# Fused SSM and SwiGLU block: the bulk loads moved to SyncE's queue in another order, the head's transposes spread over PSUM banks

## The chip, the cores and the metric

The kernel runs on one core of a Trainium2 chip. The metric is the device time of one execution in microseconds. A profiled execution gives the span from its first to its last instruction, and the profile's times count from the start of that span.

## The reference

The input x has 2048 rows (tokens) of 512 columns. Its layer norm xn goes into two branches, and the sum of both and of x is the output, in bfloat16:

```python
xn = _layernorm(x, axis=-1)
return x + _A_ref(xn, ...) + _B_ref(xn, w_gate, w_up, w_down)

# _A_ref: a diagonal state-space layer with 512 complex states
B_bar = ((Lam_bar - 1.0) / Lam)[:, None] * Bmat      # Lam_bar = exp(dt * Lam)
Bu = jnp.einsum("bld,pd->blp", x + 0j, B_bar)
h = Lam_bar[None, :] * h + Bu[:, t, :]               # over the 2048 tokens
y = 2.0 * jnp.einsum("blp,dp->bld", hseq, Cmat).real + x * Dskip

# _B_ref: w_gate and w_up are 512 x 1376, w_down is 1376 x 512
(silu(x @ w_gate) * (x @ w_up)) @ w_down
```

## The kernel before

The tokens go in four chunks of 512, each of four tiles of 128. For the matmuls that contract over the 512 columns, TensorE needs xn with columns on partitions: xnT. It is made by DMA transposes from xn, one for each tile of tokens (xT_dma, L242). The recurrence is turned into a real scan: the products with B (bproj_tile, L365, BT as weights, first four groups with the real part, then four with the imaginary part) are rotated by tables of cosines and sines on VectorE (L375 to L389), scanned there (L407), rotated back into wt, and multiplied by CF on TensorE (out_ssm, L562). CF is worked out from C (CT, L348 and L351). The gated branch is made by gate and up matmuls (L440), a product on VectorE (L459), and the down projection (out_ffn, L552, weights wd_sb). The 1376 columns are ten full groups of 128 and 96 last ones, whose weights are the tiles w_last (gate's last columns and 32 of up) and wu_last (the remaining 64 of up); they are used by gateup_last (L491, and for two chunks together in L501).

The head (L647 to L707) deals with chunk 0 before anything is normalised: x is only centred (xc), transposed by TensorE into PSUM (cT_pe, L234) and copied out by ScalarE (cT_copy, L238) as xcT, and gate and up are taken from it with tokens on the output's partitions (sw_mm, L467); the scale rstd is applied when PSUM is read (sw_out, L476 and L477). This gate and up product (g0, which lies in chunk 1's guT buffer) is transposed by four DMAs (g0_dma, L484). The head uses three weight groups, wg0/wu0 (3 x 128 columns), wg1/wu1 (4 x 128) and wg2/wu2 (3 x 128). PSUM tiles of one name take the eight banks in turn, so a ninth waits until the first has been read. tA and tB are the two banks for the head's transposes, each with two halves.

Each engine works through its instructions in the order of the program, and so do the queues that issue DMAs: SyncE's (SP), ScalarE's (ACT) and GpSimd's (POOL). The DMAs issued from SP run on one hardware queue, those from GpSimd on another (q1 and q0 in the profile). In the program's text, work for VectorE is put in a backlog (queue, with a tag and a cost for each operation); after every group of matmuls, pump lets as much of it into the program as its time pays for, and need(tag) puts in all that is left of a tag. So the place of a line in the backlog decides where VectorE's, and with it SP's and GpSimd's, instructions stand: xT_dma of a chunk is issued by the same backlog operation as the tile's norm.

Before the change, SP issues in this order: part of x and weights of group 0, wg1 and wu1, eight transposes for BT, three loads for w_last, xnT of chunk 0, xnT of chunk 1, guT's four transposes, eight for CT. GpSimd issues wg2 and wu2 among its roots for the head (L662, L669), x of chunk 1 (L686), x of chunks 2 and 3 behind chunk 1's statistics (load_x in the backlog, L704), and wu_last and wd_sb behind chunk 2's statistics (load_down, L769).

Of the kernel before, what the change touches and what calls it, by code (L numbers as in the profile page):

```python
# [23 lines left out]
def kernel(  # L24
# [17 lines left out]
    nc = tc.nc  # L42
    _, L, D = A_x.shape
    Pst = A_Lambda_re.shape[0]
    F = B_w_gate.shape[1]
# [3 lines left out]
    NT = L // 128  # L49
    NCH = L // CW  # L50
    TPC = CW // 128
    KD = D // 128
# [6 lines left out]
    LA, LB = 32, 64  # L59
    FL = (FT - 1) * 128  # L60
# [19 lines left out]
    x_v = A_x[0].rearrange("(n p) d -> p n d", p=128)  # L80
    out_v = out[0].rearrange("(n p) d -> p n d", p=128)
    wg_v = B_w_gate.rearrange("(k p) f -> p k f", p=128)
    wu_v = B_w_up.rearrange("(k p) f -> p k f", p=128)


    xall = const.tile([128, NT, D], BF16, name="xall")
# [3 lines left out]
    wg_g, wu_g = [], []  # L90
# [4 lines left out]
    w_last = const.tile([128, KD, 128], BF16, name="w_last")  # L95
# [15 lines left out]
    def load_w1(q, tiles, view, gi):  # L111
        a, b = fgroups[gi]
        q.dma_start(out=tiles[gi][:], in_=view[:, :, a * 128:min(F, b * 128)])


    def load_w1_half(q, tiles, view, gi, k0, k1):
        a, b = fgroups[gi]
        q.dma_start(out=tiles[gi][:, k0:k1, :], in_=view[:, k0:k1, a * 128:min(F, b * 128)])

    HK = KD // 2  # L120
# [7 lines left out]
    nc.scalar.preload_act_table_set("silu_and_others")  # L128
    load_w1_half(nc.sync, wu_g, wu_v, 0, HK, KD)
    nc.sync.dma_start(out=xall[:, 3, :], in_=x_v[:, 3, :])  # L130
    load_w1(nc.sync, wg_g, wg_v, 1)
    load_w1(nc.sync, wu_g, wu_v, 1)
    prm_rows = const.tile([128, 128], BF16, name="prm_rows")
    nc.gpsimd.memset(prm_rows[:], 0.0)
    for i, v in enumerate((A_Lambda_re, A_Lambda_im, A_log_dt)):
        nc.gpsimd.dma_start(out=prm_rows[i * NQ:(i + 1) * NQ, :], in_=v.rearrange("(q j) -> q j", j=128))
    for part, src in enumerate((A_B_re, A_B_im)):
        for k in range(KD):
            nc.sync.dma_start_transpose(out=BT[:, part, k, :], in_=src[:, k * 128:(k + 1) * 128])
    nc.sync.dma_start(out=w_last[:, :, 0:LB], in_=wg_v[:, :, FL + LA:F])  # L140
    nc.sync.dma_start(out=w_last[:, :, LB:LB + LA], in_=wg_v[:, :, FL:FL + LA])
    nc.sync.dma_start(out=w_last[:, :, LB + LA:128], in_=wu_v[:, :, FL:FL + LA])

    def load_x(c0, c1):
        nc.gpsimd.dma_start(out=xall[:, c0 * TPC:c1 * TPC, :], in_=x_v[:, c0 * TPC:c1 * TPC, :])

    def load_down():
        q = nc.gpsimd
        q.dma_start(out=wu_last[:], in_=wu_v[:, :, FL + LA:F])
        q.dma_start(out=wd_sb[:, 0:nfull, :], in_=B_w_down[0:nfull * 128, :].rearrange("(k p) d -> p k d", p=128))  # L150
        if nfull < FT:
            q.dma_start(out=wd_sb[0:LB, nfull, :], in_=B_w_down[FL + LA:F, :])
            q.dma_start(out=wd_sb[LB:LB + LA, nfull, :], in_=B_w_down[FL:FL + LA, :])
# [25 lines left out]
    def ln_stats(n):  # L179
        nc.vector.bn_stats(out=stats[:, n, 0, :], in_=xall[:, n, :])  # L180
        nc.vector.bn_aggr(out=mv[:, n, :], in_=stats[:, n, 0, :])  # L181

    def ln_stats_half(n, h):
        nc.vector.bn_stats(out=stats[:, n, h, :], in_=xall[:, n, h * HW:(h + 1) * HW])
        if h == 1:
            nc.vector.bn_aggr(out=mv[:, n, :], in_=stats[:, n, :, :])
# [41 lines left out]
    tB = bank((128, 2, KD, 128), BF16)  # L228
    warm = bank()

    def cT_pe(i, k0=0, k1=KD):
        tp = (tA, tA, tB, tB)[i][:, i % 2]
        for k in range(k0, k1):
            nc.tensor.transpose(out=tp[:, k, :], in_=xc[:, i, k * 128:(k + 1) * 128], identity=ident[:])  # L234

    def cT_copy(i, k0=0, k1=KD):
        tp = (tA, tA, tB, tB)[i][:, i % 2]
        nc.scalar.copy(out=xcT[:, k0:k1, i * 128:(i + 1) * 128], in_=tp[:, k0:k1, :])  # L238

    def xT_dma(n):  # L240
        c, i = divmod(n, TPC)
# [13 lines left out]
    V = nc.vector  # L255

    def prm_transpose():
        pp = tA[:, 0, 0, :]
        nc.tensor.transpose(out=pp, in_=prm_rows[:], identity=ident[:])
        V.tensor_copy(out=prm[:].rearrange("p t q -> p (t q)"), in_=pp[:, 0:3 * NQ])  # L260

# [77 lines left out]
    def c_ops():  # L339

        ops = []
        for q in range(NQ):
            for part, (one, coef) in enumerate(((0, c2re), (1, nc2re))):
                box = {}

                def pre(q=q, one=one, coef=coef, box=box):
                    box["t"] = ssm.tile([128, D], F32, name="cm", bufs=3)
                    nc.scalar.activation(out=box["t"][:], in_=CT[:, one, q, :], func=ACT.Copy, scale=coef[:, q:q + 1])  # L348

                def op(q=q, part=part, box=box):  # L350
                    V.scalar_tensor_tensor(out=CF[:, part, q, :], in0=CT[:, 1 - part, q, :], scalar=nc2im[:, q:q + 1],  # L351
                                           in1=box["t"][:], op0=ALU.mult, op1=ALU.add)
                ops.append((0.7, op, pre))
        return ops
# [127 lines left out]
    def g0_dma():  # L482
        for i in range(TPC):
            nc.sync.dma_start_transpose(out=gu_tiles[0][:, 0:FT - 1, i * 128:(i + 1) * 128], in_=g0[:, i, :])  # L484
# [3 lines left out]
    def gateup_last(c):  # L488
        ps = bank()
        for k in range(KD):  # L490
            nc.tensor.matmul(ps[:], lhsT=w_last[:, k, :], rhs=xnT[:, k, c * CW:(c + 1) * CW],  # L491
                             start=(k == 0), stop=(k == KD - 1))
        u = up_last[c] = up_p.tile([128, CW], BF16, name="ul", bufs=2)
        nc.scalar.activation(out=gu_tile(c)[0:LB + LA, FT - 1, :], in_=ps[0:LB + LA], func=ACT.Silu)
        nc.scalar.copy(out=u[LB:LB + LA, :], in_=ps[LB + LA:128])
        if c % 2 == 0:
            return
        ps = bank()
        for k in range(KD):
            for i in range(2):  # L500
                nc.tensor.matmul(ps[i * LB:(i + 1) * LB], lhsT=wu_last[:, k, :],  # L501
                                 rhs=xnT[:, k, (c - 1 + i) * CW:(c + i) * CW], start=(k == 0), stop=(k == KD - 1))
        for i in range(2):
            nc.scalar.copy(out=up_last[c - 1 + i][0:LB, :], in_=ps[i * LB:(i + 1) * LB])
            g, u = gu_tiles[c - 1 + i][0:LB + LA, FT - 1, :], up_last[c - 1 + i][0:LB + LA, :]
            products.append(lambda g=g, u=u: V.tensor_tensor(out=g, in0=g, in1=u, op=ALU.mult))
# [70 lines left out]
    def queue(tag, ops, at=None):  # L577
        ops = [[op[0], op[1], op[2] if len(op) > 2 else None, tag] for op in ops]
        if at is None:
            backlog.extend(ops)  # L580
        else:
            backlog[at:at] = ops
# [24 lines left out]
    def need(tag):  # L607

        while any(item[3] == tag for item in backlog):
            step()  # L610
# [6 lines left out]
    def dummy(n, cols):  # L617
        for _ in range(n):
            nc.tensor.matmul(warm[:, 0:cols], lhsT=one.to_broadcast([128, 128]), rhs=one.to_broadcast([128, cols]),
                             start=True, stop=True)  # L620
# [21 lines left out]
    def head_mm(which, i, k0=0, k1=KD):  # L642
        if k0 == 0:
            held[i][which] = bank()
        sw_mm(held[i][which], (G, U)[which], 0, i, k0, k1)
# [4 lines left out]
    center_by_sum(0, 0, HW)  # L650
    center_by_sum(0, HW, D)
    cT_pe(0, 0, HK)
    dummy(1, 128)
    cT_copy(0, 0, HK)
    cT_pe(0, HK, KD)
    dummy(2, 128)
    cT_copy(0, HK, KD)
    center(1, sums[:, 1:2])
    head_mm(0, 0, 0, HK)
    ln_stats(1)  # L660
    ln_rstd(1, 2)
    load_w1(nc.gpsimd, wg_g, wg_v, 2)  # L662
    cT_pe(1)
    cT_copy(1)
    head_mm(0, 0, HK, KD)
    ln_stats(2)
    center(2, mv[:, 2, 0:1])
    ln_rstd(2, 3)
    load_w1(nc.gpsimd, wu_g, wu_v, 2)  # L669
    head_mm(1, 0, 0, HK)  # L670
    ln_stats_half(0, 0)
    head_mm(0, 1)
    head_mm(1, 0, HK, KD)
    cT_pe(2)
    cT_copy(2)
    ln_stats(3)
    center(3, mv[:, 3, 0:1])
    ln_rstd(3, 4)
# [4 lines left out]
    exp_pool(dt_t[:], ldt)  # L683
    nc.gpsimd.iota(out=jidx[:], pattern=[[1, CW]], base=0, channel_multiplier=0,
                   allow_small_or_imprecise_dtypes=True)
    load_x(1, 2)  # L686
    V.tensor_scalar(out=rs0[:], in0=rstd[:, 0:1], scalar1=1.0 / D, scalar2=None, op0=ALU.mult)
    head_mm(0, 2)
    cT_pe(3)
    cT_copy(3)  # L690
    head_mm(1, 2)
    for n in range(TPC):
        norm_dve(n)
        xT_dma(n)
    params_a()
    head_mm(0, 3)
    sw_out(0, 0, *held[0])
    head_mm(1, 3)
    sw_out(0, 1, *held[1])
# [1 line left out]
    tables = table_ops()  # L701
    stats1, norm1 = ln_rest(1, False)
    queue("tables", tables[:2])
    queue("ln1", stats1 + [(0.0, lambda: load_x(2, NCH))])  # L704
    queue("tables", tables[2:6])
    queue("ln1", norm1)
    queue("tables", tables[6:])  # L707
    ln_nb(0, TPC)
    multiply(0)
    for gi in (1, 2):  # L710
# [55 lines left out]
    fwd0, back0 = ssm_ops(0)  # L766
    stats2, norm2 = ln_rest(2, True)
    queue("ssm0", fwd0[0:2] + [(1.5, params_b)])
    queue("ln2", stats2 + [(0.0, load_down)])  # L769
    queue("ssm0", fwd0[2:6])  # L770
    spread(fwd0[6:] + back0, norm2, "ssm0", "ln2")
    queue("cf", c_ops())
    g0_dma()
    gateup_last(0)
    pump(GU / 2)
    for part, src in enumerate((A_C_re, A_C_im)):
# [62 lines left out]
```

## Time and profile before

| | us |
|---|---|
| three runs, median (lowest to highest) | 191.83 (189.07 to 194.75) |
| the profiled execution | 190.17 |
| its span | 188.3 |
| TensorE busy in the span | 175.5 (93%) |
| VectorE busy | 158.2 (84%) |
| ScalarE busy | 109.3 (58%) |
| GpSimd busy | 33.3 (18%) |

Matmuls overlap one another, so the sum of TensorE's busy time is not a time at its peak rate; what can be read directly are the stretches in which it has nothing to do. In the rows of a timeline the first number is the start, the second the length, then the engine, the line, the operation with what it writes and reads, and in brackets the idle time of the engine before it and what ended it. SPq, ACTq and POOLq are the instructions that issue DMAs. In the rows on DMAs the last number is the median time from issue to landing.

### The profile page before, as it was taken

How to read it: one execution, taken by the hardware profiler on the slowest of the kernel's cores; microseconds unless marked ns; L12 is line 12 of the kernel's file. 1: busy time of each engine (PE TensorE's matmuls, PEld its weight loads, DVE VectorE, ACT ScalarE, POOL GpSimd, SP SyncE). 2: the span in 40 equal slices, each digit the busy share in tenths (PEclk: the TensorE clock that was granted, in tenths of full speed). 3: DMA queues.
4: the chain of work that ended last, by engine and by line, in shares of the span. 5: the costliest groups of instructions: out<-in, count | busy, mean ns of one | idle time of the engine just before them, and what ended most of it. 6: DMA issues, size and time to landing. Idle time of an engine off the chain costs nothing.

```text
span 188.3 us, 2432 instructions
## 1 busy us (share of the span) xinstructions
PE 175.5 (93%) x865; PEld 81.4 (43%) x865; DVE 158.2 (84%) x258; ACT 109.3 (58%) x186; POOL 33.3 (18%) x44
## 2 busy tenths in 40 slices
PE   7999969990799999999999999999999999999993
PEld 2544624330244444444444444444444444444742
DVE  3988999595299989899999999999999997798033
ACT  4369987971268977902589666003677687772000
POOL 5780130008200000002610000003300002507000
PEclk9999999997599999999999999999999999999999
DMA  6999768985991490001724000002700000994512
GB/s 183 325 232 266 101 159 203 179 167 101 300 113 28 83 335 0 3 0 9 79 42 96 3 0 0 0 0 28 85 4 0 0 0 7 153 177 48 65 49 68
DMA packets 32412, 17.37 MB, mean 92 GB/s; under 512 B 25248, under 2 KB 31424, under 8 KB 32368
## 3 DMA queue, kind: packets, MB, share of 16 engines
q1 hardware_dynamic: 26896, 9.48, 24.8%
q0 software_dynamic: 4528, 7.12, 21.3%
q10 hardware_dynamic: 976, 0.62, 1.1%
q8 instruction: 7, 0.11, 0.2%
q14 instruction: 5, 0.04, 0.1%
HBM read 8.03 MB, written 5.24 MB: 70 GB/s over the span
## 4 chain that ended last, share of the span: by engine, by line
PE 76%; DVE 11%; ACT 5%; DMA 3%; POOL 1%; issue 1%; ACTq 1%; DVEq 0%
PE ps L440 28%; PE ps L552 20%; PE ps L562 15%; PE ps L365 11%; DVE stats L180 4%; DMA wu_last<-in_B_w_up_dram 2%; PE ps L501 2%; POOL rstd L190 1%; DMA xnT<-CF 1%; DVE pm L375 1%; ACT u L477 1%; ACT guT L476 1%; DVE mv L181 1%; PE ps L491 1%; DVE CF L198 1%
## 5 line engine op out<-in xcount | busy, mean ns | idle before, releaser
L552 PE MATMUL ps<-wd_sb,guT 128*128 128x512 bf16 (+3 forms) x198 | 38.8, 355 | 0.0
L440 PE MATMUL ps<-xnT,wg 128*128 128x512 bf16 x120 | 31.6, 387 | 0.0
L440 PE MATMUL ps<-xnT,wu 128*128 128x512 bf16 x120 | 30.8, 379 | 0.0
L365 PE MATMUL ps<-xnT,BT 128*128 128x512 bf16 x128 | 28.3, 379 | 2.1 <-DMA xnT<-CF 1.8
L407 DVE TENSOR_TENSOR_SCAN g<-r_t,car,u 128x512 bf16<-128x512 f32 x24 | 28.9, 1262 | 0.0
L562 PE MATMUL ps<-CF,wt 128*128 128x512 bf16 (+2 forms) x144 | 28.3, 355 | 0.0
L552 PEld LDWEIGHTS <-guT 128*128 128x128 bf16 (+1 forms) x198 | 18.5, 98 | 19.9
L569 POOL DMA_DIRECT2D out_dram<-res x12 | 10.5, 1046 | 84.2 <-ACT res L568 78.2
L367 ACT CAST u<-ps 128x512 bf16<-128x512 f32 x32 | 18.5, 585 | 7.1 <-PE ps L365 7.1
L568 ACT CAST res<-ps 128x512 bf16<-128x512 f32 x12 | 7.0, 585 | 26.7 <-PE ps L562 26.7
L454 ACT ACTIVATE guT<-ps 128x512 bf16<-128x512 f32 x30 | 17.9, 598 | 5.8 <-PE ps L440 5.8
L455 ACT CAST u<-ps 128x512 bf16<-128x512 f32 x30 | 17.6, 585 | 5.4 <-PE ps L440 5.3
L365 PEld LDWEIGHTS <-BT 128*128 128x128 bf16 x128 | 12.4, 98 | 17.6 <-issue 2.9
L562 PEld LDWEIGHTS <-wt 128*128 128x128 bf16 x144 | 13.5, 98 | 14.3
L440 PEld LDWEIGHTS <-wg 128*128 128x128 bf16 x120 | 11.7, 99 | 15.2 <-issue 1.8
L440 PEld LDWEIGHTS <-wu 128*128 128x128 bf16 x120 | 11.8, 98 | 14.5 <-issue 0.5
L524 ACT ACTIVATE xr<-xall,nb,rstd 128x512 bf16<-128x512 bf16 x16 | 11.9, 804 | 2.7 <-DVE xall L532 1.4
L190 POOL TENSOR_TENSOR rstd<-ve,neg_half 128x1 f32<-128x1 f32 (+1 forms) x7 | 7.3, 1039 | 29.7 <-DVE ve L189 29.7
L467 PEld LDWEIGHTS <-CF 128*128 128x128 bf16 x96 | 9.0, 98 | 8.1 <-ACT CF L238 1.0
L375 DVE TENSOR_TENSOR pm<-u,c 128x2048 bf16<-128x2048 bf16 x8 | 9.8, 1221 | 2.0 <-ACT c L292 1.9
L467 PE MATMUL ps<-wg,CF 128*128 128x384 bf16 (+1 forms) x48 | 10.8, 344 | 0.0
L459 DVE TENSOR_TENSOR guT<-guT,u 128x1024 bf16<-128x1024 bf16 x15 | 10.0, 675 | 0.9 <-ACT u L455 0.9
(117 smaller groups left out, 207.5 us busy)
## 6 DMA issues: line engine op xcount, KB each, us to landing
out_dram<-in_A_x_dram SPq DMA_DIRECT2D x1, 1536.0 KB, 7.1
out_dram<-res POOLq DMA_DIRECT2D x12, 128.0 KB, 3.2
out_dram<-xall POOLq DMA_DIRECT2D x3, 512.0 KB, 6.7
wd_sb<-in_B_w_down_dram POOLq DMA_DIRECT2D x1, 1280.0 KB, 8.5
xall<-in_A_x_dram POOLq DMA_DIRECT2D x1, 1024.0 KB, 6.3
wg<-in_B_w_gate_dram SPq DMA_DIRECT2D x1, 512.0 KB, 5.6
wu<-in_B_w_up_dram SPq DMA_DIRECT2D x1, 512.0 KB, 6.5
xall<-in_A_x_dram POOLq DMA_DIRECT2D x1, 512.0 KB, 6.3
```

Of the source, the lines that this page charges most:

```text
L365: nc.tensor.matmul(ps[:], lhsT=BT[:, part, k, q * 128:(q + 1) * 128], rhs=xnT[:, k, c * CW:(c + 1) * CW], start=(k == 0), stop=(k == KD - 1))
L367: nc.scalar.copy(out=u_tiles[c][:, part, q, :], in_=ps[:])
L375: V.tensor_tensor(out=t[:], in0=flat(src()[:, i]), in1=flat(tab[:]), op=ALU.mult)
L407: V.tensor_tensor_scan(out=g()[:, part, q, :], data0=r_t[:, q:q + 1].to_broadcast([128, CW]), data1=u_tiles[c][:, part, q, :], initial=ini ...
L440: nc.tensor.matmul(ps[:fs, lo:hi], lhsT=wslice(groups, fi, k), rhs=xnT[:, k, c * CW + lo:c * CW + hi], start=(k == 0), stop=(k == KD - 1))
L454: nc.scalar.activation(out=guT[:fs, fi, :], in_=psg[:fs], func=ACT.Silu)
L455: nc.scalar.copy(out=u_pair[c][:fs, fi % 2, :], in_=psu[:fs])
L467: nc.tensor.matmul(ps[:, 0:(b - a) * 128], lhsT=xcT[:, k, i * 128:(i + 1) * 128], rhs=groups[gi][:, k, :], start=(k == 0), stop=(k == KD - 1))
L524: nc.scalar.activation(out=box["xr"][:], in_=xall[:, n, :], func=ACT.Identity, scale=rstd[:, n:n + 1], bias=nb[:, n:n + 1])
L552: nc.tensor.matmul(o[:], lhsT=gu_tiles[c][:fsz[fi], fi, i * 128:(i + 1) * 128], rhs=wd_sb[:fsz[fi], fi, lo:hi], start=(fi == 0), stop=False)
L562: nc.tensor.matmul(o[:], lhsT=w_tiles[c][:, part, q, i * 128:(i + 1) * 128], rhs=CF[:, part, q, lo:hi], start=False, stop=(part == 1 and q ...
L569: nc.gpsimd.dma_start(out=out_v[:, n, lo:hi], in_=res[:, lo:hi], accum_op=ALU.add)
```

## The change

All bulk loads but four small ones go to SP's queue. Behind wg0 and wu0 it issues the weights of groups 1 and 2 as eight half loads, x of chunk 1, the four transposes of BT's real part, xnT of chunk 0, the four of BT's imaginary part, xnT of chunk 1, x of chunks 2 and 3 (load_late), guT's transposes, wd_sb (load_down), and CT's transposes. GpSimd issues w_last's three loads and wu_last behind params_a (load_last). Chunk 1's norms come two table operations earlier in the backlog, and need("ln1") stands ahead of load_late. In the head the first tile's transposes go half to tA and half to tB, the second and third tile's to the other halves, the fourth's to tA; the matmuls of the first tile come after the second tile's transposes, and one dummy matmul stays of three.

```diff
     load_w1_half(nc.sync, wu_g, wu_v, 0, HK, KD)
     nc.sync.dma_start(out=xall[:, 3, :], in_=x_v[:, 3, :])
-    load_w1(nc.sync, wg_g, wg_v, 1)
-    load_w1(nc.sync, wu_g, wu_v, 1)
+    for gi in (1, 2):
+        for tiles, view in ((wg_g, wg_v), (wu_g, wu_v)):
+            load_w1_half(nc.sync, tiles, view, gi, 0, HK)
+            load_w1_half(nc.sync, tiles, view, gi, HK, KD)
...
-    for part, src in enumerate((A_B_re, A_B_im)):
+    nc.sync.dma_start(out=xall[:, TPC:2 * TPC, :], in_=x_v[:, TPC:2 * TPC, :])
+
+    def load_bt(part):
+        src = (A_B_re, A_B_im)[part]
         for k in range(KD):
             nc.sync.dma_start_transpose(out=BT[:, part, k, :], in_=src[:, k * 128:(k + 1) * 128])
-    nc.sync.dma_start(out=w_last[:, :, 0:LB], in_=wg_v[:, :, FL + LA:F])
-    nc.sync.dma_start(out=w_last[:, :, LB:LB + LA], in_=wg_v[:, :, FL:FL + LA])
-    nc.sync.dma_start(out=w_last[:, :, LB + LA:128], in_=wu_v[:, :, FL:FL + LA])
-
-    def load_x(c0, c1):
-        nc.gpsimd.dma_start(out=xall[:, c0 * TPC:c1 * TPC, :], in_=x_v[:, c0 * TPC:c1 * TPC, :])
+
+    load_bt(0)
+
+    def load_last():
+        q = nc.gpsimd
+        q.dma_start(out=w_last[:, :, 0:LB], in_=wg_v[:, :, FL + LA:F])
+        q.dma_start(out=w_last[:, :, LB:LB + LA], in_=wg_v[:, :, FL:FL + LA])
+        q.dma_start(out=w_last[:, :, LB + LA:128], in_=wu_v[:, :, FL:FL + LA])
+        q.dma_start(out=wu_last[:], in_=wu_v[:, :, FL + LA:F])
+
+    def load_late():
+        nc.sync.dma_start(out=xall[:, 2 * TPC:NT, :], in_=x_v[:, 2 * TPC:NT, :])
 
     def load_down():
-        q = nc.gpsimd
-        q.dma_start(out=wu_last[:], in_=wu_v[:, :, FL + LA:F])
+        q = nc.sync
...
+    def cT_tile(i, k):
+        return (((tA, 0) if k < HK else (tB, 0)), (tA, 1), (tB, 1), (tA, 0))[i]
+
     def cT_pe(i, k0=0, k1=KD):
-        tp = (tA, tA, tB, tB)[i][:, i % 2]
+        t, h = cT_tile(i, k0)
...
     cT_pe(0, 0, HK)
-    dummy(1, 128)
     cT_copy(0, 0, HK)
     cT_pe(0, HK, KD)
-    dummy(2, 128)
     cT_copy(0, HK, KD)
     center(1, sums[:, 1:2])
-    head_mm(0, 0, 0, HK)
+    dummy(1, 128)
+    cT_pe(1)
+    cT_copy(1)
+    head_mm(0, 0)
     ln_stats(1)
     ln_rstd(1, 2)
-    load_w1(nc.gpsimd, wg_g, wg_v, 2)
-    cT_pe(1)
-    cT_copy(1)
-    head_mm(0, 0, HK, KD)
     ln_stats(2)
     center(2, mv[:, 2, 0:1])
     ln_rstd(2, 3)
-    load_w1(nc.gpsimd, wu_g, wu_v, 2)
+    head_mm(0, 1)
+    ln_stats_half(0, 0)
     head_mm(1, 0, 0, HK)
-    ln_stats_half(0, 0)
-    head_mm(0, 1)
-    head_mm(1, 0, HK, KD)
     cT_pe(2)
     cT_copy(2)
+    head_mm(1, 0, HK, KD)
...
-    load_x(1, 2)
...
-    head_mm(0, 2)
+    head_mm(0, 2, 0, HK)
     cT_pe(3)
     cT_copy(3)
+    head_mm(0, 2, HK, KD)
...
     params_a()
-    head_mm(0, 3)
+    load_last()
+    load_bt(1)
+    for i in range(2):
+        head_mm(0, 3, i * HK, (i + 1) * HK)
...
     queue("tables", tables[:2])
-    queue("ln1", stats1 + [(0.0, lambda: load_x(2, NCH))])
-    queue("tables", tables[2:6])
+    queue("ln1", stats1)
+    queue("tables", tables[2:4])
     queue("ln1", norm1)
-    queue("tables", tables[6:])
+    queue("tables", tables[4:])
...
-    queue("ln2", stats2 + [(0.0, load_down)])
+    queue("ln2", stats2)
...
+    need("ln1")
+    load_late()
     g0_dma()
+    load_down()
     gateup_last(0)
```

More of the change, by code (lines that the diff above doesn't have):

```diff
@@ L229 @@
     warm = bank()
+    def cT_tile(i, k):
+        return (((tA, 0) if k < HK else (tB, 0)), (tA, 1), (tB, 1), (tA, 0))[i]
     def cT_pe(i, k0=0, k1=KD):
-        tp = (tA, tA, tB, tB)[i][:, i % 2]
+        t, h = cT_tile(i, k0)
         for k in range(k0, k1):
-            nc.tensor.transpose(out=tp[:, k, :], in_=xc[:, i, k * 128:(k + 1) * 128], identity=ident[:])
+            nc.tensor.transpose(out=t[:, h, k, :], in_=xc[:, i, k * 128:(k + 1) * 128], identity=ident[:])
     def cT_copy(i, k0=0, k1=KD):
-        tp = (tA, tA, tB, tB)[i][:, i % 2]
-        nc.scalar.copy(out=xcT[:, k0:k1, i * 128:(i + 1) * 128], in_=tp[:, k0:k1, :])
+        t, h = cT_tile(i, k0)
+        nc.scalar.copy(out=xcT[:, k0:k1, i * 128:(i + 1) * 128], in_=t[:, h, k0:k1, :])
     def xT_dma(n):
@@ L257, in prm_transpose @@
     def prm_transpose():
-        pp = tA[:, 0, 0, :]
+        pp = tA[:, 1, 0, :]
         nc.tensor.transpose(out=pp, in_=prm_rows[:], identity=ident[:])
```

## The prediction

> **What bounds the kernel now.** I read the page first, then TensorE's timeline, then the chain of waits, then five-microsecond windows.
>
> ```profile
> span 188.3 us, 2432 instructions
> ...
> PE 175.5 (93%) x865; PEld 81.4 (43%) x865; DVE 158.2 (84%) x258; ACT 109.3 (58%) x186; POOL 33.3 (18%) x44
> ```
>
> TensorE works 93% of the span, so time can only come out of its few gaps. Its timeline names them (start, length, what; idle before it in brackets):
>
> ```profile
> 4.83 0.27 PE L234 MATMUL ps<-ident,CF 128*128 128x128 bf16 x2 [0.40 <-ACT CF L238]
> ...
> 23.17 0.81 PE L467 MATMUL ps<-wu,CF 128*128 128x384 bf16 x4
> 25.79 7.07 PE L365 MATMUL ps<-xnT,BT 128*128 128x512 bf16 x32 [1.80 <-DMA xnT<-CF]
> ...
> 34.00 7.07 PE L365 MATMUL ps<-xnT,BT 128*128 128x512 bf16 x32 [0.28 <-DMA xnT<-xn]
> ...
> 48.18 1.92 PE L501 MATMUL ps<-xnT,wu_last 128*64 128x512 bf16 x8 [6.25 <-DMA wu_last<-in_B_w_up_dram]
> ...
> 68.11 7.07 PE L365 MATMUL ps<-xnT,BT 128*128 128x512 bf16 x32
> ...
> 84.53 7.07 PE L562 MATMUL ps<-CF,wt 128*128 128x512 bf16 x32
> ```
>
> One gap is large: 6.25 us before the eight matmuls on wu_last. The chain shows where it comes from and what follows it:
>
> ```profile
> 44.81 3.32 DMA wu_last<-in_B_w_up_dram
> ...
> 48.18 1.92 PE ps L501 x8
> 50.10 18.18 PE ps L440 x80
> ...
> 92.47 17.27 PE ps L440 x80
> ...
> 133.92 0.98 PE ps L501 x8
> ```
>
> The load is issued only at 44.81, because it sits in load_down behind the statistics of chunk 2 on GpSimd's in-order queue. The matmuls after it are slow as well: 1.92 us against 0.98 for the same eight at 133.92, and 18.18 against 17.27 for the same eighty. The windows (busy time of PE, PEld, DVE, ACT, POOL, then the granted clock, DMA share, GB/s) say why:
>
> ```profile
> 5.00:10.00 5.00, 4.97 (x40) 2.90 (x38) 4.41 (x16) 1.78 (x4) 3.50 (x6) 1.00 1.10 310
> ...
> 20.00:25.00 5.00, 3.98 (x25) 2.17 (x23) 4.79 (x11) 4.99 (x10) 2.15 (x2) 1.00 0.85 126
> ...
> 45.00:50.00 5.00, 1.82 (x8) 0.55 (x8) 0.22 (x1) 0.00 (x0) 3.21 (x5) 0.50 0.81 200
> ```
>
> The long gap halves the granted clock (0.50); the 1.80 gap at 24 to 25.8 leaves it at 1.00 in its window.
>
> **The change part by part.**
>
> *wu_last and w_last early, on GpSimd.* The four small loads go out behind the power of params_a, which is GpSimd's last work before the root of chunk 1's statistics near 23:
>
> ```profile
> 12.77 1.04 POOL L263 TENSOR_TENSOR r_t<-e_t,dre 128x4 f32<-128x4 f32 x1
> ```
>
> Four issues of some 0.8 us end at 17; with the worst landing below (8.5 us) all is there by 26, against a need after the first L365 group (33 us) for w_last and at 42 for wu_last. The gap of 6.25 goes, and with it the half clock: 1.92 - 0.98 = 0.94 and 18.18 - 17.27 = 0.91. Together 8.10 us. Nothing else stands behind it there: L501's other operand, xnT of chunks 0 and 1, has fed L365 since 34.00. This is the main term.
>
> *SyncE's queue.* All other loads and transposes now go through it in one order, so I walk that order with the issue times of before:
>
> ```profile
> 3.63 0.51 SPq L113 DMA_DIRECT2D wu<-in_B_w_up_dram  x1
> 4.18 6.17 SPq L139 DMA_TRANSPOSE BT<-in_A_B_re_dram  x4
> 10.39 5.95 SPq L139 DMA_TRANSPOSE BT<-in_A_B_im_dram  x4
> ...
> 18.20 6.30 SPq L242 DMA_TRANSPOSE xnT<-CF  x4
> 27.51 5.12 SPq L242 DMA_TRANSPOSE xnT<-xn  x4
> 32.72 5.99 SPq L484 DMA_TRANSPOSE guT<-guT  x4
> 38.76 5.42 SPq L778 DMA_TRANSPOSE CT<-in_A_C_re_dram  x4
> 44.22 5.84 SPq L778 DMA_TRANSPOSE CT<-in_A_C_im_dram  x4
> 59.27 5.95 SPq L242 DMA_TRANSPOSE xnT<-xn  x4
> ```
>
> Two issues at 3.15 to 4.18 become nine (eight weight halves and x of chunk 1), 0.51 each: BT's real part starts at 7.75 and ends near 13.9, where the normalised x of chunk 0 has been ready since 12. Its four transposes (5.12 when undisturbed, 6.30 as shown) end at 19.1 to 20.3 and land by 23, where before they were issued until 24.5. TensorE leaves the head at 23.98 (23.17 + 0.81), so its 1.80 wait goes. BT's imaginary part, now behind them, is issued until 25.1 to 26.3. The rows of landing (KB each, median us from issue to landing) price the rest:
>
> ```profile
> wd_sb<-in_B_w_down_dram POOLq DMA_DIRECT2D x1, 1280.0 KB, 8.5
> xall<-in_A_x_dram POOLq DMA_DIRECT2D x1, 1024.0 KB, 6.3
> ...
> xnT<-xn SPq DMA_TRANSPOSE x12, 2.5
> ...
> BT<-in_A_B_im_dram SPq DMA_TRANSPOSE x4, 6.5
> ...
> guT<-guT SPq DMA_TRANSPOSE x4, 3.5
> CT<-in_A_C_re_dram SPq DMA_TRANSPOSE x4, 2.9
> CT<-in_A_C_im_dram SPq DMA_TRANSPOSE x4, 7.7
> ```
>
> BT's imaginary part is needed after half of the first L365 group, 23.98 + 3.45 = 27.4. Its last transpose is issued near 23.8 to 25.0; at 2.9 to landing (CT's real part, with no bulk load beside it) it is there at 26.7 to 27.9, at 6.5 (as now, with bulk) at 31.5. I take 2.9, for by then the bulk loads of the start are through: some 3.7 MB at the 310 GB/s shown, from 2 us on, are done at 14. So 0, with 4.1 as the upper end.
>
> *Chunk 1's norms ahead.* The turns of the second pair and a product move behind them:
>
> ```profile
> 25.74 0.88 DVE L279 TENSOR_SCALAR pm<-jidx,ws 128x512 f32<-128x512 f32 x2
> ...
> 27.08 1.37 DVE L198 TENSOR_SCALAR xn<-xall,mv,rstd 128x512 bf16<-128x512 bf16 x4
> ```
>
> Norms that began at 27.08 can begin at 25.8 (27.08 - 25.74, less the tiny nb, is 1.27). SyncE is free for their transposes at 25.1 to 26.3, wanted from 26.24. So they land 1.27 earlier: L365 of chunk 1 starts at 32.73 instead of 34.00. TensorE would be there at 23.98 + (34.00 - 0.28 - 25.79) = 31.91, so 0.82 us of a wait stays where 0.28 was: of the 1.80 gained in front only 1.27 arrives. Bounds: 0 (BT late instead) and 1.8.
>
> *load_late, load_down and the transposes behind them.* SyncE leaves chunk 1's transposes at 31.4, issues x of chunks 2 and 3 until 32, guT's four until 38.0, wd's three until 39.7, CT's eight (5.42 + 5.84) until 51.0, then chunk 2's xnT. x lands 6.3 later, at 38, as DVE's statistics of chunk 2 want it (39.4 before). Chunk 2's xnT meets TensorE at the 68.11 row, which now starts 8.10 + 1.27 = 9.37 earlier, at 58.74. Its last operand comes from ScalarE:
>
> ```profile
> 61.89 1.52 ACT L203 ACTIVATE xn<-xall,nb,rstd 128x512 bf16<-128x512 bf16 x2
> ```
>
> 63.4 - 9.4 = 54.0; SyncE's fourth issue is at 51.0 + 3 x 1.3 = 54.9, landing 2.5 later at 57.4: 1.3 us to spare. But guT stands behind 1 MB on its own queue, and CT behind 1.4 MB. If issue is not held, that costs 0; if SyncE is held as long as these 2.45 MB take at 310 GB/s, 7.9, so 6.6 at TensorE. The nearest row is BT's real part, issued behind some 1.9 MB of loads: 6.17 for four where CT's rows give 5.42, and 5.04 at the 1.26 of the undisturbed ones; about 1.1 held. Twice that, less 1.3, is 0.9. I take 0.9.
>
> The Trainium skill (DMA: Bandwidth & Descriptors, section "Queues, rings and completion order") says that each DMA engine takes turns among its queues packet by packet; by it, transposes beside a bulk load on GpSimd's queue keep getting turns, and behind one on their own queue they get none, which would make the sum the 6.6 case. The trace agrees with the turns only in part: CT's imaginary part, beside wd on the other queue, landed after 7.7 us against 2.9 for the real part.
>
> *The head.* The bank edit takes away the 0.40 wait in front of 4.83. In exchange head_mm(1, 2) gets the bank (tA) from which cT_copy(3) has just read, some 0.3 us. I count 0, bounds -0.4 and +0.4. The dropped dummies filled gaps only.
>
> *VectorE.* With TensorE 9.4 us ahead it could be late for out_ssm(0), the 84.53 row.
>
> ```profile
> 35.03 1.23 DVE L375 TENSOR_TENSOR pm<-u,c 128x2048 bf16<-128x2048 bf16 x1 [1.93 <-ACT c L292]
> 50.75 0.42 DVE L506 TENSOR_TENSOR guT<-guT,ul 96x512 bf16<-96x512 bf16 x1 [5.53 <-ACT ul L504]
> 76.92 4.06 DVE L351 SCALAR_TENSOR_TENSOR CF<-CT,nc2im,cm 128x512 bf16<-128x512 bf16 x6 [0.34 <-ACT cm L348]
> ```
>
> CF is done at 80.98; the 5.53 wait goes as well, and, I estimate, half of the 1.93 (a sine that stands behind ScalarE's copies of the first L365 group, which end 1.8 earlier): 74.5, against 84.53 - 9.37 = 75.2. Just in time; bounds 0 and 0.3.
>
> Sum: 8.10 + 1.27 - 0.9 = 8.47. The execution profiled took 190.17 us, 1.87 of it outside the span: 190.17 - 8.47 = 181.7. It stands 1.66 below the median of the three runs and 1.1 above the lowest, so I forecast 182.0.
>
> **The rivals.**
>
> A, bulk in front of transposes: SyncE is held, chunk 2's xnT is late. For it: the queue is one, the 6.17 and 6.30 rows. Against: SyncE never waited a whole load. It decides from 1.3 us of hold; at 7.9 it gives 190.17 - 9.37 + 6.6 = 187.4, at half the hold (about 4) 183.5. This is also the page's rule.
>
> B, BT's imaginary part late: landing at 31.5, 4.1 late at TensorE; L365 of chunk 1 then starts at 31.91 + 4.1 = 36.0 instead of 32.73, 3.3 lost: 185.0. For it: 6.5 is what this tile took; against: bulk is through by then.
>
> C, slower: each transpose waits for the one ahead to land before the next is issued, because the queue is full behind the bulk loads. guT 4 x 3.5, CT 8 x 2.9, xnT 4 x 2.5 make 47.2 us in place of 22.5: 24.7 later, less 1.3, 23.4 at TensorE: 204. It decides from 9.4 + 1.3 = 10.7 us of hold. Against: the rows show the next issue long before a landing.
>
> D, it doesn't do what it says: something else keeps L501 until 48, and earlier work only lengthens that wait: 190.2. Against: its other operand is there from 34.00.
>
> **How the numbers follow.** Forecast 0.58 (its own range 179.5 to 184); A 0.22, B 0.10, D 0.06, C 0.04. The range, 179.5 to 187.5, takes in A at its price and B; its low end has no 0.9 and a run somewhat below the profiled one. A measurement of this kernel tells about 2% from no change, 188.0 here: faster 0.57 + 0.20 + 0.09 = 0.86; no change 0.09 (D, ends of A and B); slower 0.05 (C and a hold near it).
>
> **What would show it.** Right: no gap at L501, its eight matmuls at 0.98, clock 1.00 throughout, L365 of chunk 1 near 32.7, TensorE without a gap from there on, or one under 2 us at L365 of chunk 2. Wrong: a gap over 3 us at L365 of chunk 2 (A) or in the middle of L365 of chunk 0 (B), SyncE issues of one transpose over 2 us in a row, or a new wait before out_ssm(0) on VectorE.

## The result and the profile after

The changed kernel takes 182.51 us (median of four runs, 182.23 to 182.76); the kernel before, now with four runs, 190.71 us (189.07 to 194.75). The ratio is 0.960, 95% interval 0.952 to 0.968: faster. Ratios here leave out runs over 1.5% above the fastest of their kernel, as the one of 194.75. The execution profiled took 182.76 us with a span of 181.0, where the sum of the prediction stood at 181.7 and 179.8. The forecast was 182.0, in a range from 179.5 to 187.5.

The head of the page after:

```profile
span 181.0 us, 2419 instructions
...
PE 173.1 (96%) x847; PEld 81.5 (45%) x863; DVE 157.8 (87%) x258; ACT 108.6 (60%) x186; POOL 30.5 (17%) x40
...
PEclk9999999999999999999999999999999999999999
```

TensorE's timeline after the change (the file is longer, so L365 is now L378, L501 is L514, L440 is L453, L562 is L575):

```profile
23.73 7.07 PE L378 MATMUL ps<-xnT,BT 128*128 128x512 bf16 x31
...
32.73 7.08 PE L378 MATMUL ps<-xnT,BT 128*128 128x512 bf16 x31 [1.07 <-DMA xnT<-xn]
...
40.60 1.05 PE L514 MATMUL ps<-xnT,wu_last 128*64 128x512 bf16 x8
...
60.81 7.07 PE L378 MATMUL ps<-xnT,BT 128*128 128x512 bf16 x32 [1.78 <-DMA xnT<-xn]
...
77.23 2.97 PE L575 MATMUL ps<-CF,wt 128*128 128x512 bf16 x13
```

The gap before the wu_last matmuls is gone and so is the 1.80 wait before the first L378 group; the wait at chunk 1 has grown from 0.28 to 1.07, and a new one of 1.78 stands at chunk 2. The clock stays up. From the row of chunk 2 to the end the length is the same: 181.0 - 60.81 = 120.2 us after, 188.3 - 68.11 = 120.2 before. So all of the 7.3 us lies ahead of that row. SyncE's queue tells where the new wait comes from:

```profile
14.30 6.08 SPq L255 DMA_TRANSPOSE xnT<-CF  x4
20.44 5.17 SPq L144 DMA_TRANSPOSE BT<-in_A_B_im_dram  x4
26.13 5.32 SPq L255 DMA_TRANSPOSE xnT<-xn  x4
31.51 0.57 SPq L156 DMA_DIRECT2D xall<-in_A_x_dram  x1
32.18 8.47 SPq L497 DMA_TRANSPOSE guT<-guT  x4
...
42.42 1.45 SPq L163 DMA_DIRECT2D wd_sb<-in_B_w_down_dram  x1
43.92 5.07 SPq L793 DMA_TRANSPOSE CT<-in_A_C_re_dram  x4
49.03 5.17 SPq L793 DMA_TRANSPOSE CT<-in_A_C_im_dram  x4
54.29 5.14 SPq L255 DMA_TRANSPOSE xnT<-xn  x4
...
49.19 1.52 ACT L213 ACTIVATE xn<-xall,nb,rstd 128x512 bf16<-128x512 bf16 x2
...
52.64 1.52 ACT L213 ACTIVATE xn<-xall,nb,rstd 128x512 bf16<-128x512 bf16 x2
```

(The last two rows are ScalarE's: the norms of chunk 2.) guT's four transposes, behind the load of 1 MB, take 8.47 us to issue where they took 5.99 (the first two 2.65 and 2.74 us, the others 1.37 and 1.44), and wd's three loads occupy SyncE from 40.7 to 43.9. Chunk 2's xnT is issued from 54.29 and not from about 51, though ScalarE has its first norms ready near 51 and the last near 54 (52.64 + 1.52).

### The profile page after: what moved, and what is told of

It is laid out like the page before. It is cut to its first block, busy times and chain, and to the rows that moved or that the text cites. A ratio compares the mean times of both kernels' runs of the same rounds, so it can differ in the third digit from the quotient of the medians.

```text
span 181.0 us, 2419 instructions
## 1 busy us (share of the span) xinstructions
PE 173.1 (96%) x847; PEld 81.5 (45%) x863; DVE 157.8 (87%) x258; ACT 108.6 (60%) x186; POOL 30.5 (17%) x40
## 4 chain that ended last, share of the span: by engine, by line
PE 81%; DVE 9%; DMA 4%; ACT 3%; issue 1%; POOL 0%; DVEq 0%
PE ps L453 28%; PE ps L565 21%; PE ps L575 15%; PE ps L378 12%; DMA xnT<-xn 3%; PE ps L480 2%; PE ps L504 1%; DVE stats L190 1%; DVE pm L301 1%; DMA xall<-in_A_x_dram 1%; DVE guT L493 1%; ACT guT L489 1%; ACT u L490 1%; PE ps L514 1%; DVE CF L208 1%
## 5 line engine op out<-in xcount | busy, mean ns | idle before, releaser
L565 PE MATMUL ps<-wd_sb,guT 128*128 128x512 bf16 (+4 forms) x195 | 38.6, 355 | 0.2
L378 PE MATMUL ps<-xnT,BT 128*128 128x512 bf16 x126 | 28.2, 379 | 3.0 <-DMA xnT<-xn 2.9
L453 PE MATMUL ps<-xnT,wg 128*128 128x512 bf16 x120 | 30.8, 379 | 0.1
L453 PE MATMUL ps<-xnT,wu 128*128 128x512 bf16 x114 | 30.0, 379 | 0.2
L575 PE MATMUL ps<-CF,wt 128*128 128x512 bf16 (+2 forms) x140 | 28.1, 355 | 0.2
L378 PEld LDWEIGHTS <-BT 128*128 128x128 bf16 x128 | 12.4, 98 | 18.3 <-issue 2.2
L575 PEld LDWEIGHTS <-wt 128*128 128x128 bf16 x144 | 13.4, 97 | 14.3
L453 PEld LDWEIGHTS <-wu 128*128 128x128 bf16 x120 | 11.7, 98 | 14.2
L453 PEld LDWEIGHTS <-wg 128*128 128x128 bf16 x120 | 11.6, 98 | 14.5 <-issue 0.8
L578 DVE TENSOR_TENSOR xall<-ps,xall 128x512 bf16<-128x512 f32 (+2 forms) x6 | 3.1, 513 | 8.7 <-remote 6.3
```

The costliest lines, as they stand in the source:

```text
L378: nc.tensor.matmul(ps[:], lhsT=BT[:, part, k, q * 128:(q + 1) * 128], rhs=xnT[:, k, c * CW:(c + 1) * CW], start=(k == 0), stop=(k == KD - 1))
L453: nc.tensor.matmul(ps[:fs, lo:hi], lhsT=wslice(groups, fi, k), rhs=xnT[:, k, c * CW + lo:c * CW + hi], start=(k == 0), stop=(k == KD - 1))
L565: nc.tensor.matmul(o[:], lhsT=gu_tiles[c][:fsz[fi], fi, i * 128:(i + 1) * 128], rhs=wd_sb[:fsz[fi], fi, lo:hi], start=(fi == 0), stop=False)
L575: nc.tensor.matmul(o[:], lhsT=w_tiles[c][:, part, q, i * 128:(i + 1) * 128], rhs=CF[:, part, q, lo:hi], start=False, stop=(part == 1 and q ...
```

## The experiments

**wu_last alone.** One edit to the kernel before:

```diff
     def load_down():
         q = nc.gpsimd
-        q.dma_start(out=wu_last[:], in_=wu_v[:, :, FL + LA:F])
...
     params_a()
+    nc.gpsimd.dma_start(out=wu_last[:], in_=wu_v[:, :, FL + LA:F])
     head_mm(0, 3)
```

> The kernel before with one edit: wu_last alone is loaded early, on GpSimd behind params_a; all other loads stay where they were. Theory (the early wu_last carries the whole gain): the 6.25 us gap and the half clock go, 8.1 us, the waits of 1.80 and 0.28 stay, and L365 of chunk 2 has no wait, since SyncE is through with CT at 50: span near 180.2, 182.1 us. Rival (the new order of SyncE's queue carries part of it): over 184 us, with a new gap at L365 of chunk 2 or before out_ssm(0).

Measured: 184.14 us (182.3 to 186.65), ratio 0.964 (0.953 to 0.974); the profiled execution 183.9, span 182.1.

```profile
5.50 0.85 PE L466 MATMUL ps<-wg,CF 128*128 128x384 bf16 x2
...
26.79 7.07 PE L364 MATMUL ps<-xnT,BT 128*128 128x512 bf16 x31 [1.01 <-ACT guT L475]
35.81 7.07 PE L364 MATMUL ps<-xnT,BT 128*128 128x512 bf16 x31 [1.08 <-DMA xnT<-xn]
43.67 1.05 PE L500 MATMUL ps<-xnT,wu_last 128*64 128x512 bf16 x8
61.93 7.07 PE L364 MATMUL ps<-xnT,BT 128*128 128x512 bf16 x32
```

Behind chunk 1 it does what the theory says: from chunk 1's L364 to chunk 2's it is 61.93 - 35.81 = 26.12 us, against 68.11 - 34.00 = 34.11 before: 7.99 gained, with no wait at chunk 2. What is missing of the 180.2 was lost in the head: this execution's first matmuls took 0.85 us for two where the profile before shows 0.49, and the chain was 1.8 us late at 35.81. The edit doesn't touch them, and the fastest of the four executions, 182.3 us, has a span of 180.5, near the 180.2. One line therefore carries the main term; the total alone would have left the question open.

**All but wu_last.** The changed kernel with wu_last back behind chunk 2's statistics:

```diff
-        q.dma_start(out=wu_last[:], in_=wu_v[:, :, FL + LA:F])
+
+    def load_wu_last():
+        nc.gpsimd.dma_start(out=wu_last[:], in_=wu_v[:, :, FL + LA:F])
...
-    queue("ln2", stats2)
+    queue("ln2", stats2 + [(0.0, load_wu_last)])
```

> The changed kernel with wu_last issued on GpSimd behind chunk 2's statistics, as before the change. Theory: the gap before the wu_last matmuls comes back with 5.8 to 6.6 us (issue near 44, landing 3.3 later, TensorE there at 41), the half clock with it, and the 1.78 wait at chunk 2 vanishes behind it: 187 to 190 us. Rival (the order carries the gain): under 185 us.

Measured, in one run: 192.3 us, span 190.5.

```profile
49.73 1.92 PE L516 MATMUL ps<-xnT,wu_last 128*64 128x512 bf16 x8 [8.82 <-DMA wu_last<-in_B_w_up_dram]
70.33 7.07 PE L380 MATMUL ps<-xnT,BT 128*128 128x512 bf16 x32
...
wu_last<-in_B_w_up_dram POOLq DMA_DIRECT2D x1, 64.0 KB, 5.4
```

The gap comes back, with 8.82 larger than expected, since the load took 5.4 us to land instead of 3.3; SyncE's w_down loads (1.4 MB) now move at the same time, which is the likely reason. The half clock is back too (1.92), and the wait at chunk 2 has vanished behind it. In this one run all the rest of the change together brings nothing by itself: what is gained ahead of this gap only makes it longer.

**w_down on GpSimd.**

```diff
     def load_down():
-        q = nc.sync
+        q = nc.gpsimd
...
-    queue("ln2", stats2)
+    queue("ln2", stats2 + [(0.0, load_down)])
...
     g0_dma()
-    load_down()
```

> The changed kernel with w_down's three loads back on GpSimd, behind chunk 2's statistics. Theory (the 1.78 wait at chunk 2 is the time in which SyncE is held): SyncE's 3.2 us for them go, chunk 2's transposes start near 51, the wait goes: 180.9 us, span 179.2. Rival (bulk slows transposes through the shared DMA engines, whichever queue it is on): CT's imaginary part lands after 7 us or more, as before the change, the wait of 1.8 stays or grows: 182.5 us or more.

Measured: 182.66 us (182.48 to 185.93), ratio 0.960 (0.956 to 0.964). No gain over the changed kernel.

```profile
40.77 5.79 SPq L792 DMA_TRANSPOSE CT<-in_A_C_re_dram  x4
46.60 7.12 SPq L792 DMA_TRANSPOSE CT<-in_A_C_im_dram  x4
53.83 5.14 SPq L255 DMA_TRANSPOSE xnT<-xn  x4
...
60.29 7.07 PE L378 MATMUL ps<-xnT,BT 128*128 128x512 bf16 x32 [1.28 <-ACT u L468]
```

SyncE starts CT 3.2 us earlier, at 40.77, but needs 5.79 and 7.12 for its two parts, where it took 5.07 and 5.17, and is only 0.5 us ahead at chunk 2's xnT. TensorE's wait there is 1.28 by its timeline. My theory, that only SyncE's own queue matters, fell short here, and the rival came near: a bulk load on another queue can hold transposes as well. Only the 7.12 shows it, since GpSimd issues the loads from 44.16 on; the run with w_down last, below, has no load beside CT and shows 5.77 and 5.17.

**Late x on ScalarE's queue.**

```diff
     def load_late():
-        nc.sync.dma_start(out=xall[:, 2 * TPC:NT, :], in_=x_v[:, 2 * TPC:NT, :])
+        nc.scalar.dma_start(out=xall[:, 2 * TPC:NT, :], in_=x_v[:, 2 * TPC:NT, :])
```

> The changed kernel with the load of x of chunks 2 and 3 issued from ScalarE's queue at the same place of the program, so that it moves beside guT's transposes, but not ahead of them on their queue. Theory (SyncE is held since its own queue is full of the bulk load): guT's four issues take 6.0 us instead of 8.5, SyncE is 3 us ahead, the 1.78 wait goes: 180.9 us. Rival (the shared engines are what slows guT): guT's issues stay near 8.5 us, the wait between 1.2 and 1.8: 182 us or more. VectorE may wait up to 2 us for x in both.

Measured: 183.86 us (182.63 to 184.88), ratio 0.966 (0.958 to 0.974); span 182.9.

```profile
31.30 9.88 SPq L497 DMA_TRANSPOSE guT<-guT  x4
...
60.99 8.75 PE L378 MATMUL ps<-xnT,BT 128*128 128x512 bf16 x32 [2.21 <-DMA xnT<-xn]
```

With the load off its queue, guT's issue is slower still, 9.88 us, and SyncE comes to CT no earlier (43.99 against 43.92). So a load in SyncE's own queue is not needed to hold it: the theory fails. guT's transposes are held while x's load moves, on either queue. The Trainium skill (DMA: Bandwidth & Descriptors, section "Queues, rings and completion order") lets each DMA engine take turns among its queues; taking turns did not keep these transposes moving at their pace. The four executions are of two kinds: 184.65 (the one profiled) and 184.88 us have a granted clock of 0.991 over the span, 182.63 and 183.07 have 1.00. So most of the loss against the changed kernel goes with a fall of the clock, which the profile shows behind the 2.21 wait (last section).

**w_down last.** The bulk load should then go to a time at which no transpose is waiting. w_down is needed only by out_ffn(0), at 67.7 in the changed kernel:

```diff
     g0_dma()
-    load_down()
...
     gateup_chunk(1)
+    load_down()
```

> The changed kernel with w_down's three loads still on SyncE, but behind the xnT transposes of chunk 2, so that no bulk load moves beside CT's and these transposes. Theory, as the runs so far leave it (transposes are held while a bulk load moves, on whichever queue): CT's eight take 10.3 us and end near 51, chunk 2's xnT is issued as its norms come (until 55.5) and lands before 58, the 1.78 wait at chunk 2 goes, w_down lands near 63, before out_ffn(0) at 66: span 179.1, 180.8 us. Rival (SyncE's issue itself is slow, whatever moves): the wait stays above 1 us, 182 us.

Measured: 180.65 us (180.36 to 180.83), ratio 0.950 (0.947 to 0.953); span 179.0. Each step came near what was expected, CT's eight with 11.0 us for 10.3:

```profile
40.62 5.77 SPq L792 DMA_TRANSPOSE CT<-in_A_C_re_dram  x4
46.44 5.17 SPq L792 DMA_TRANSPOSE CT<-in_A_C_im_dram  x4
51.71 5.16 SPq L255 DMA_TRANSPOSE xnT<-xn  x4
56.92 0.57 SPq L160 DMA_DIRECT2D wd_sb<-in_B_w_down_dram  x1
...
32.64 7.08 PE L378 MATMUL ps<-xnT,BT 128*128 128x512 bf16 x31 [0.92 <-DMA xnT<-xn]
40.52 1.05 PE L514 MATMUL ps<-xnT,wu_last 128*64 128x512 bf16 x8
58.78 7.07 PE L378 MATMUL ps<-xnT,BT 128*128 128x512 bf16 x32
```

(The first four rows are SyncE's timeline, the others TensorE's.) TensorE enters chunk 2's group at 58.78 without a wait; w_down lands 6.6 us after its issue, by 64, ahead of its use at 65.7. SyncE comes to chunk 2's xnT 2.6 us earlier than in the changed kernel (51.71 against 54.29): the 3.2 us in which it issued w_down's loads are gone, and CT's eight took 0.7 us longer (11.0 against 10.3). So the gain is SyncE's own issue time; that w_down had held CT's transposes in the changed kernel is not shown, the rows speak against it. This version beats both kernels, by 1.9 us the changed one.

**w_down last, and chunk 1's norms first.** In addition:

```diff
-    queue("tables", tables[2:4])
     queue("ln1", norm1)
-    queue("tables", tables[4:])
+    queue("tables", tables[2:])
```

> As the kernel with w_down's loads last, and chunk 1's norms right behind its statistics, ahead of all further table work. Theory: SyncE is free at 25.6 and is now limited by its own queue, chunk 1's xnT lands 0.5 us earlier, the 1.07 wait falls to 0.6; VectorE stands 1.5 us for the root, which out_ssm(0) does not see (3.5 us to spare): span 178.6, 180.3 us. Rival (VectorE's stand reaches TensorE): 181 us or more, with a wait before out_ssm(0) or chunk 2's xnT.

Measured: 180.44 us (179.83 to 180.97), ratio 0.949 (0.946 to 0.953); span 178.7, the wait at chunk 1 down to 0.52:

```profile
32.31 7.08 PE L378 MATMUL ps<-xnT,BT 128*128 128x512 bf16 x31 [0.52 <-DMA xnT<-xn]
```

The profile shows the step; the 0.2 us between the two medians is within their spreads and is not shown by the times.

**The old head.** The changed kernel with the head's old order, dummies and banks (the wg2 and wu2 loads stay on SyncE):

```diff
-    def cT_tile(i, k):
-        return (((tA, 0) if k < HK else (tB, 0)), (tA, 1), (tB, 1), (tA, 0))[i]
...
     cT_pe(0, 0, HK)
+    dummy(1, 128)
     cT_copy(0, 0, HK)
     cT_pe(0, HK, KD)
+    dummy(2, 128)
     cT_copy(0, HK, KD)
     center(1, sums[:, 1:2])
-    dummy(1, 128)
-    cT_pe(1)
-    cT_copy(1)
-    head_mm(0, 0)
+    head_mm(0, 0, 0, HK)
...
```

> The changed kernel with the head as it was: its order, its three dummies and the two transposes' banks in one. Theory (the head ends 0.25 us later, and the 1.07 wait for chunk 1's xnT takes that up): same as the changed kernel, 182.5 us, within 0.3. Rival (the head's order decides how long TensorE runs slowly after the start, as in the run with wu_last alone, where the first matmuls took twice as long until 9 us): executions spread from 182.3 to 185 us, median near 184.

Measured: 182.68 us (182.5 to 184.01), ratio 0.962 (0.959 to 0.966): the same as the changed kernel. The head ends at 24.24 instead of 23.73, and the wait at chunk 1 shrinks from 1.07 to 0.79:

```profile
24.24 7.07 PE L375 MATMUL ps<-xnT,BT 128*128 128x512 bf16 x31
32.96 7.08 PE L375 MATMUL ps<-xnT,BT 128*128 128x512 bf16 x31 [0.79 <-DMA xnT<-xn]
```

**wu_last early and the new head, the old order of loads.** This is the kernel with wu_last alone, with the changed kernel's head:

```diff
     cT_pe(0, 0, HK)
-    dummy(1, 128)
     cT_copy(0, 0, HK)
...
+    dummy(1, 128)
+    cT_pe(1)
+    cT_copy(1)
+    head_mm(0, 0)
     ln_stats(1)
     ln_rstd(1, 2)
     load_w1(nc.gpsimd, wg_g, wg_v, 2)
...
```

> The kernel before with wu_last early and the new head, SyncE's queue as before the change. Theory (the early wu_last carries the gain and the new order gives and takes about as much): span near 180.2, 182.1 us. Rival (the new head keeps TensorE's clock up): executions within 0.5 us of one another, where those of wu_last alone ranged from 182.3 to 186.65; if the spread stays, it isn't the head.

Measured: 182.37 us, median of six (182.21 to 191.65), ratio 0.959 (0.956 to 0.963): as the theory said, and as fast as the whole change.

```profile
25.07 7.07 PE L367 MATMUL ps<-xnT,BT 128*128 128x512 bf16 x31 [0.92 <-ACT guT L478]
34.37 7.07 PE L367 MATMUL ps<-xnT,BT 128*128 128x512 bf16 x31 [1.36 <-DMA xnT<-xn]
42.23 1.05 PE L503 MATMUL ps<-xnT,wu_last 128*64 128x512 bf16 x8
60.49 7.07 PE L367 MATMUL ps<-xnT,BT 128*128 128x512 bf16 x32
```

Chunk 1 starts 1.6 us later than in the changed kernel, chunk 2 0.3 us earlier: what the new order of loads gains at chunk 1 it gives back at chunk 2. The new head does not by itself keep the slow start away: in this profile its first eight matmuls on wg took 1.99 us, in the changed kernel's 1.83, and in the run with all but wu_last 1.46. Whether it keeps away one as long as in the run with wu_last alone is left open: all executions but the one of 191.65 lie within 0.4 us here, but those of the old head with the new order lie near 182.6 too, but for one of 184.01 and one of 182.98.

## Why the prediction was right

The forecast held by its own steps, and the size of one, the hold of SyncE, was off.

- *wu_last and the clock, 8.10.* From chunk 1's group to chunk 2's without a wait is 26.14 us (58.78 - 32.64, w_down last), 26.12 (wu_last alone), 34.11 before: 7.97 and 7.99. Right, and shown by undoing it and by doing it alone.
- *The 1.80 wait, of which 1.27 arrives.* Chunk 1's group starts at 32.73, as forecast to the hundredth; SyncE was free at 25.6 and the norms came at 25.70, so the chain was limited by VectorE as I had it. The wait left is 1.07 instead of 0.82, as the head ended 0.25 earlier. One stop was not foreseen: SyncE stood 0.9 us among the half loads, from 4.09 to 4.97, and BT's real part started at 8.57 instead of 7.75. It cost nothing, since chunk 0's last xnT still landed near 22, ahead of the head's end.
- *The head, 0.* It ended 0.25 us earlier than before, and 0.51 earlier than in the run with the old head. The wait for xnT of chunk 1 took up 0.28 of the 0.51, and the times of the two kernels (182.51 and 182.68) are the same.
- *BT's imaginary part, 0.* It took 2.7 us to landing, and no wait stands in the middle of chunk 0's group. Rival B did not occur.
- *The hold of SyncE, 0.9.* This term was mis-sized. With w_down last chunk 2's group starts at 58.78, in the changed kernel at 60.81, of which 0.09 is chunk 1's later start: 1.94. I had taken the 1.1 us held behind the loads of the start, twice, less 1.3 to spare. In fact SyncE came to chunk 2's xnT 3.3 us late (54.29 against 51.0), in the main from three differences: guT's issue grew by 2.5 us, wd's three took 3.2 for 1.7, and CT gave 1.0 back (10.3 for 11.3). So rival A was at work, with 1.9 of its 6.6 us at TensorE, and one of the signs that I had named for being wrong showed: two of guT's transposes in a row took over 2 us to issue (2.65 and 2.74). The mechanism was also put too simply. The place in SyncE's queue is not what decides, since x holds guT's transposes from ScalarE's queue and w_down holds CT's from GpSimd's (7.12 us for 5.17). And w_down ahead of CT on SyncE's own queue did not hold CT at all; its price there was the issue of its three loads, 3.2 us, which took 2.1 when they came last. Why x holds guT there and w_down does not hold CT stays open.
- *VectorE, just in time.* CF was done at 73.7 (rows below) against 77.2 at out_ssm(0), 3.5 us to spare instead of 0.7, since a wait of 0.88 for a copy of ScalarE's went too and TensorE came 1.9 later. (The first row is from the profile before, the others from the one after.)

```profile
68.93 0.69 DVE L459 TENSOR_TENSOR guT<-guT,u 128x1024 bf16<-128x1024 bf16 x1 [0.88 <-ACT u L455]
...
69.62 4.06 DVE L364 SCALAR_TENSOR_TENSOR CF<-CT,nc2im,cm 128x512 bf16<-128x512 bf16 x6 [0.35 <-ACT cm L361]
73.60 1.22 DVE L388 TENSOR_TENSOR pm<-u,c 128x2048 bf16<-128x2048 bf16 x1
```

The sum was 8.47 and the span fell by 7.3; 1.04 of the difference is the hold, the rest the main term's 0.13. That the median of 182.51 lies so near 182.0 is partly luck: it owes something to the 0.3 us that I had added for the profiled execution's place among the runs.

## What to carry to other kernels

Look first for a small load that stands late in an in-order queue behind work it doesn't need: moving that one line, with the new head, was worth as much as the whole change (182.37 and 182.51 us). Count a bulk load's price twice: in the time of the queue that issues it (3.2 us for w_down's three loads), and in the transposes that are issued while it moves, which may be held even if it is on another queue (by 2.0 and 3.9 us here). Put it where none is waiting, as late as its use allows. When an early part is made faster, ask which transfer the next wait ends on: here 1.80 us gained became 1.27 at the next group, and was lost again at the one after it.

## What the runs showed that I had not expected

A transpose's issue can be slowed by a load on another queue: guT's four took 5.99 us alone, 8.47 behind 1 MB on their own queue and 9.88 beside it on ScalarE's. It is not a general rule: CT's eight took 10.3 us behind 1.4 MB on their own queue and 11.0 with no load there.

The clock can fall after a shorter gap than I had allowed for. Waits of 1.80 and 1.78 us left it at 1.00; after the 2.21 of the run with late x on ScalarE's queue it was granted 0.74 in the window from 60 to 64 us, and the group took 8.75 us instead of 7.07:

```profile
60.00:64.00 4.00, 3.01 (x10) 1.23 (x11) 4.00 (x11) 0.91 (x3) 0.00 (x0) 0.74 0.95 346
```

The Trainium skill (TensorE: Matmul & The Clock Gate, section "Part 1: The HAM clock gate") gives about 3.4 us of idle time in a free-running window; the 6.25 us gap agrees, the 2.21 us one is shorter than that. The trace's record of the clock keeps each state for whole multiples of 3.413 us; here half clock stands from 61.93 to 65.34. Of the 3.41 us up to 61.93 TensorE had been idle for 2.21; in the changed kernel its record puts such a boundary at 60.74, and of the 3.41 us up to there it had been idle for 1.71, without a fall. So, as I infer from these cases, the idle time within one such stretch counts, and the limit lies between 1.71 and 2.21 us.

The first matmuls can run at half pace far into the head: the 0.85 us rows of the run with wu_last alone, which cost that execution about 1.8 us (the row that stands at 7.84 in the profile before stands at 9.64). The windows print a granted clock of 1.00 there, but that is no reading: the trace's record of the clock begins only at 9.03 us, with full clock, and the next row, at 9.09, is back at 0.49. In the changed kernel's profile the record begins at 6.13, in the one before at 3.90. When it begins differs between executions of the same head, and what decides it is not shown.
